# An AFNO kernel: the gathers of the remainder rows of the first two chunks issued by GpSimd instead of SyncE, with the buffers on the right at other addresses

## The chip, the cores and the metric

The kernel runs on one core of a Trainium2 chip. The metric is the time of one execution on the device in microseconds (us), as the median of several executions. Five engines work beside each other and are named as in the profile: PE (TensorE, matmuls), DVE (VectorE), ACT (ScalarE), POOL (GpSimd) and SP (SyncE, which here only issues DMAs). An engine works through its instructions in program order; semaphores tie the engines and the DMAs to one another.

## What is computed

One block of a network on x of 4096 positions and 640 channels (f32): layer norm with a scale and shift taken from a condition vector c, a spectral mixing (AFNO: Fourier transform over the positions, a two-layer complex MLP on the channels of each frequency, soft shrink, inverse transform), and then a SwiGLU feed-forward part. Shortened:

```python
mod = (silu(c) @ w_mod).reshape(1, 6, 1, -1)          # sa, ca, ga, sb, cb, gb
h = layernorm(x) * (1 + ca) + sa
z = rfft2(h over (1, 4096)).reshape(..., 4, 160)      # 4 blocks of 160 channels
hr = relu(z.real @ w1[0] - z.imag @ w1[1] + b1[0])
hi = relu(z.imag @ w1[0] + z.real @ w1[1] + b1[1])
o_r = softshrink(hr @ w2[0] - hi @ w2[1] + b2[0], 0.01)
o_i = softshrink(hi @ w2[0] + hr @ w2[1] + b2[1], 0.01)
x = x + ga * irfft2(o_r + 1j * o_i)
h = layernorm(x) * (1 + cb) + sb
x = x + gb * ((silu(h @ w_gate) * (h @ w_up)) @ w_down)   # 640 -> 1728 -> 640
```

## The kernel before

**Stages.** The AFNO part takes up to about 340 us of the execution, the feed-forward part the rest. The transform of 4096 points is split in two steps, A and B, with a reordering through memory between them. In step A eight tiles t of x (`xa0` to `xa7`, in the pool `xp` on the right side of the on-chip memory) are normalised and multiplied by the first transform's matrix. The results overwrite the `xa` tiles. Step B works on eight chunks ch of frequencies. Chunk 0's tile `g0` is moved directly from the `xa` tiles (`move_g`, L313 to L315, some of these DMAs on POOL); for the others the `xa` tiles are copied in bulk to DRAM (`write_s1`, L353 to L355) and read back as `g1` to `g7` (`load_g`, L301 to L310) along with a table `tb` (`load_tb`).

**A chunk.** For a chunk, `stage_b` (L593) makes step B's matmuls in five groups of 128 channels, t = 0 to 4. The first four groups hold the first 128 channels of each of the four blocks; the fifth holds the 32 channels that remain of each block, four times 32. `evac_b` (L602) takes each group out of PSUM as two parts, a rounded high half by ACT (L606) and the low half by DVE (L607), in a tile `z{ch}_{t}`. The matmuls of the first MLP layer want a block's 32 remaining rows in another arrangement: real and imaginary, high and low half beside each other on 128 partitions. `move_r` (L615 to L619) makes that by four DMAs of 128 KB, one for each block, from `z{ch}_4` into the tile `rz{ch}`. `stage_l1` (L621, matmuls at L646) is the first layer of one block: weights `w1a` and `w1b` on `z{ch}_{b}`, `w1c` on `rz{ch}`. For chunk 0, block 0 all products with `w1a` and `w1b` are issued ahead of the first with `w1c`. ACT and DVE make the high and low halves `h` of the result (L656 to L658), and `u` and `r` of its remainder. `stage_l2` (L682, matmuls at L698) is the second layer with `w2a`, `w2b` and `w2c`, one block behind the first. The inverse transform follows (`stage_i`, L734) and its results go to DRAM by DMAs of POOL (L748, from tiles `co`).

**The second layer's weights** are also split in high and low halves: `weights_high` (ACT at L282, or POOL at L280), `weights_low` (DVE, L285) and `weights_rest` (POOL, L527, the low half as a difference). Each of `w2a`, `w2b` and `w2c` is made in two pieces by several of these. They lie in the pool `p2` on the right, in the place that the `xa` tiles had before, so writing them has to wait for the copies out of the `xa` tiles that lay there.

**What sets the order.** In the AFNO part the order is that of the code (a manual schedule), on every engine. SP issues almost all DMAs, and each of its DMAs uses one of eight semaphores in turn and waits for the DMA eight places before it, so that at most eight are under way. At the place in question the code has, in this order: the bulk copies of the tiles (L490 to L505, with `load_g(1)` and `load_tb(1)` among them), loads of `idn` (L507), `tx` (L508) and `bx` (L530); `stage_b` of chunk 0 for t = 4, 0 and 1; two `weights_high` on ACT; `evac_b(0, 4)`; `move_r(0)` (L774); `evac_b` of t = 0 and 1; the rest of the second layer's weights; and then a loop over p = 4 ch + b, in which `stage_l1` of one block, `stage_b` and `evac_b` of the next chunk, and `stage_l2` of the block before follow one another. `z1_4` and `move_r(1)` come at p = 2.

```python
evac_b(0, 4)
move_r(0)
for b in range(2):
    evac_b(0, b)
weights_low(*prep2[0])
weights_rest(1)
for n in (2, 3):
    weights_high(*prep2[n], pool)
weights_rest(3)
weights_high(*prep2[5], pool)
weights_rest(5)
```

Here `prep2` lists the pieces of the weights: 0 and 1 are of `w2a`, 2 and 3 of `w2b`, 4 and 5 of `w2c`. After the AFNO part, the feed-forward part is put in order by a planner; its instructions are the same before and after.

Of the kernel before, what the change touches and what calls it, by code (L numbers as in the profile page):

```python
# [6 lines left out]
F32 = mybir.dt.float32  # L7
F32R = mybir.dt.float32r
# [5 lines left out]
P = 128  # L14
D = 640
# [157 lines left out]
def body(tc, x, w1, b1, w2, b2, wg, wu, wd, c, wm, k_fa, k_tb, k_tx, k_bm, k_bx, k_ga, k_ge, k_id, out, dbg=None):  # L173
    nc = tc.nc
    pe, act, dve, pool = nc.tensor, nc.scalar, nc.vector, nc.gpsimd
    mm = pe.matmul

    def f32(ap):
        return ap.bitcast(F32)
# [21 lines left out]
    with ExitStack() as top:  # L201
# [35 lines left out]
        with ExitStack() as af:  # L237
            wp = af.enter_context(tc.tile_pool(name="wp", bufs=1, side="right"))
            w1a = wp.tile([P, NB, 640], F32R, tag="w1a", name="w1a")
            w1b = wp.tile([P, NB, 640], F32R, tag="w1b", name="w1b")  # L240
            w1c = qp.tile([P, NB, 640], F32R, tag="wq", name="w1c")
            bm = wp.tile([P, 2, 64], F32, name="bm")
            tx = wp.tile([P, 2], F32, name="tx")
            lp = af.enter_context(tc.tile_pool(name="lp", bufs=1))
            fa = lp.tile([P, 130], F32, name="fa")
# [244 lines left out]
            hp = af.enter_context(tc.tile_pool(name="hp", bufs=1, reuse_waits="tile"))  # L490
# [18 lines left out]
            p2 = af.enter_context(tc.tile_pool(name="p2", bufs=1, side="right", reuse_waits="tile"))  # L509
# [75 lines left out]
            zs = {}  # L585
            pbs = {}
            rzs = {}
            hss = {}

            def width(ch):  # L590
                return 258 if ch == CE else 256
# [9 lines left out]

            def evac_b(ch, t):  # L602
                pb = pbs[ch, t]
                z = lp.tile([P, 2, 2, 258], F32R, tag="z" if t < 4 else "zr", bufs=4 if t < 4 else 1, name=f"z{ch}_{t}")
                zs[ch, t] = z
                act.activation(z[:, 0, :, 0:256], pb, AF.Identity, scale=ca1[:, t:t + 1])  # L606
                dve.scalar_tensor_tensor(z[:, 1, :, 0:256], pb, ca1[:, t:t + 1],  # L607
                                         f32(z[:, 0, :, 0:256]), op0=OP.mult, op1=OP.subtract)
                if ch == CE:
                    pool.tensor_copy(z[:, 0, :, 0:257:256], f32(edge[:, 0, t]))  # L610
                    pool.tensor_copy(z[:, 1, :, 0:257:256], f32(edge[:, 1, t]))
                    pool.tensor_copy(z[:, :, :, 257], zero[:, 0, 0])


            def move_r(ch):  # L615
                rzs[ch] = hp.tile([P, NB, 258], F32R, tag="rz", bufs=2, name=f"rz{ch}")
                NN = width(ch)
                for b in range(NB):
                    nc.sync.dma_start(f32(rzs[ch][:, b, :NN]), f32(zs[ch, 4][32 * b:32 * b + 32, :, :, :NN]))  # L619

            def stage_l1(ch, b):  # L621
                NN = width(ch)
# [148 lines left out]
            for n in (1, 0):  # L771
                weights_high(*prep2[n])
# [4 lines that stand above are left out]
# [31 lines left out]
            def load_first_rows(lo, hi, q, e=slice(0, D)):  # L808
                for k in range(2):
                    q.dma_start(cf[k][lo:hi, :, e], s2[lo:hi, 2 * k:2 * k + 2, e])  # L810
# [4 lines left out]
            for p in range(LAST + 1):  # L815
                ch, b = p // 4, p % 4
# [11 lines left out]
                for q in todo:  # L828
                    stage_b(*q)
                    evac_b(*q)  # L830
                    if q[1] == 4:
                        move_r(q[0])
# [38 lines left out]
                elif p == LAST - 1:  # L871
                    load_first_rows(0, rb - 16, nc.sync)


            def load_first():
                x2 = fx.tile([P, 4, D], F32, tag="gx", bufs=2, name="x2_0")
                nc.sync.dma_start(x2, xv[:, 0:4, :])
                x2s[0] = x2
# [146 lines left out]
        with ExitStack() as ff:  # L1025
# [42 lines left out]
            bufs = {"R": 2, "h1": 1, "wb": 2, "wt": 2, "pc": 4, "px": 2, "gt": 2, "ho": 2, "h32": 1, "gx": 2}  # L1068
# [1324 lines left out]
            mv, rs, _ = fst[3]  # L2393
# [18 lines left out]
            for t in range(NS):  # L2412
                for n in range(NW):
                    if sum_at(n) == t:
                        a, b = sum_w(n)
# [81 lines left out]
```

## Time and profile before

| | us |
|---|---|
| median of 3 executions | 1436.88 |
| lowest and highest of them | 1433.94 and 1438.77 |
| the profiled execution, its own time | 1432.89 |
| the span of its profile | 1431.1 |

The profile is of one execution. Its span runs from the first to the last recorded instruction. A window view cuts the span into stretches and gives for each engine the busy time and, in brackets, the number of instructions; after that the granted clock of PE (1.00 is full speed), the share of the 16 DMA engines' time that was used, and the rate in GB/s. Cut along the kernel's stages:

```profile
0.00:36.00 36.00, 24.75 (x51) 9.69 (x52) 31.05 (x104) 25.52 (x39) 19.94 (x55) 1.00 0.95 375
36.00:60.00 24.00, 22.55 (x94) 13.20 (x92) 20.61 (x41) 18.42 (x35) 16.62 (x18) 1.00 0.90 319
60.00:81.40 21.40, 0.10 (x2) 0.02 (x1) 0.00 (x0) 0.00 (x0) 8.18 (x7) 0.56 0.96 348
81.40:124.00 42.60, 42.60 (x322) 41.91 (x323) 28.05 (x55) 26.34 (x58) 0.00 (x0) 0.94 0.44 125
124.00:340.00 216.00, 213.85 (x1592) 184.21 (x1591) 154.59 (x292) 146.85 (x311) 56.82 (x101) 1.00 0.68 207
340.00:1431.00 1091.00, 1080.57 (x6413) 1046.38 (x6411) 788.40 (x1287) 501.85 (x1019) 517.39 (x517) 1.00 0.80 277
```

The columns are PE, PEld (PE's loading of weights, which runs beside its matmuls), DVE, ACT and POOL. Rows of a timeline give start and duration, engine, line, operation, the tiles `out<-in` without their numbers, shapes, how many instructions are drawn together (x4), and in square brackets the idle time before and what ended it. `SPq` stands for SP's issuing of DMAs, in which the wait for a free semaphore is included; a transfer lands later.

### The profile page before, as it was taken

Reading aid. Unit: us, or ns where it says so; the run is one execution under the profiler, and the core shown is the slowest. Engines: PE = TensorE matmul, PEld = TensorE weight load, DVE = VectorE, ACT = ScalarE, POOL = GpSimd, SP = SyncE. Lnnn points to the kernel's source line nnn. Section 1 sums busy time; section 2 is a strip of 40 time slices with the busy share of each in tenths; the row PEclk is TensorE's granted clock in tenths of the full one; section 3 lists DMA queues with packets and bytes.
Section 4 is the critical chain, followed back from the end, with each engine's and each line's share of the span. In section 5 each row is a group of like instructions: output and inputs, shape, how many; then the busy total and the mean of one; then the engine's idle time right before and its main releaser. Section 6 shows DMA issues by size and latency. Waiting matters only on the chain. (4 is left out here: it accounts for less than half of the span.)

```text
span 1431.1 us, 23688 instructions
## 1 busy us (share of the span) xinstructions
PE 1384.4 (97%) x8466; PEld 1295.4 (91%) x8466; DVE 1022.7 (71%) x1777; ACT 719.0 (50%) x1458; POOL 619.0 (43%) x696
## 2 busy tenths in 40 slices
PE   6679999999999999999999999999999999999998
PEld 2379989967988988899999999999999999999998
DVE  8547666779798698737796848687669757375654
ACT  7547777736555455426463536355255525152441
POOL 5601221137786586416454716345344525052241
PEclk9879999999999999999999999999999999999999
DMA  9956666776698998798968898877999766966634
GB/s 374 330 174 190 210 180 221 196 243 214 222 328 293 338 323 290 273 388 299 341 208 307 319 345 282 296 265 238 368 336 319 233 233 243 348 220 201 205 122 147
DMA packets 175623, 381.35 MB, mean 266 GB/s; under 512 B 22705, under 2 KB 86385, under 8 KB 173490
## 3 DMA queue, kind: packets, MB, share of 16 engines
q1 hardware_dynamic: 166098, 363.55, 73.9%
q0 software_dynamic: 7104, 13.67, 3.3%
q10 hardware_dynamic: 2304, 2.62, 0.5%
q8 instruction: 67, 1.10, 0.3%
q14 instruction: 50, 0.41, 0.1%
HBM read 269.29 MB, written 96.80 MB: 256 GB/s over the span
## 5 line engine op out<-in xcount | busy, mean ns | idle before, releaser
L1400 DVE TENSOR_TENSOR wb<-r,wb 128x768 fp32r<-128x768 f32 (+3 forms) x170 | 174.7, 1038 | 16.1 <-ACT wb L1393 15.8
L2008 PE MATMUL pw<-h,wt 128*128 128x384 f32 x412 | 139.4, 338 | 0.6 <-ACT s_y L2027 0.6
L2010 PE MATMUL pw<-h,wt 128*128 128x384 f32 x412 | 138.3, 336 | 0.0
L2009 PE MATMUL pw<-h,wt 128*128 128x384 f32 x412 | 138.1, 335 | 0.0
L2309 PE MATMUL pc<-wq,L 128*128 128x320 f32 x846 | 132.7, 309 | 0.6 <-DVE x L2266 0.6
L1393 ACT ACTIVATE wb<-r 128x768 fp32r<-128x768 f32 (+3 forms) x168 | 104.6, 639 | 57.0 <-PE pw L2021 41.7
L2068 POOL TENSOR_TENSOR sg<-s_x,sg 128x384 f32<-128x384 f32 x24 | 29.8, 1242 | 234.2 <-DVE s_x L2034 234.2
L2309 PEld LDWEIGHTS pc<-wq,L 128*128 128x128 f32 x846 | 126.3, 188 | 0.8 <-DVE x L2266 0.8
L2088 DVE TENSOR_TENSOR L<-sg,L 128x384 fp32r<-128x384 f32 x144 | 102.9, 738 | 27.4 <-ACT L L2084 26.9
L748 POOL DMA_DIRECT2D s<-co x56 | 33.5, 602 | 185.2 <-ACT co L746 184.6
L2027 ACT ACTIVATE s_x<-pw 128x384 f32<-128x384 f32 x52 | 25.6, 492 | 166.2 <-PE pw L2010 165.2
L2008 PE MATMUL pw<-h,wb 128*128 128x384 f32 x312 | 105.0, 336 | 0.8 <-DVE x L2266 0.8
L2009 PE MATMUL pw<-h,wb 128*128 128x384 f32 x312 | 104.4, 335 | 0.0
L2010 PE MATMUL pw<-h,wb 128*128 128x384 f32 x312 | 104.4, 335 | 0.0
L1931 PE MATMUL pg<-ht,wb 128*128 128x512 f32 x260 | 102.5, 394 | 0.0
L2079 POOL TENSOR_TENSOR sg<-sg,sg 128x384 f32<-128x384 f32 x72 | 92.2, 1280 | 23.2 <-DVE L L2088 19.9
L1932 PE MATMUL pg<-ht,wb 128*128 128x512 f32 x260 | 101.9, 392 | 0.0
L2309 PE MATMUL pe<-wq,L 128*128 128x320 f32 x648 | 101.7, 309 | 0.0
L1933 PE MATMUL pg<-ht,wb 128*128 128x512 f32 x260 | 101.7, 391 | 0.0
L2225 PE MATMUL pd<-wq,a 128*128 128x320 f32 x632 | 96.9, 310 | 0.0
L2309 PEld LDWEIGHTS pe<-wq,L 128*128 128x128 f32 x648 | 96.6, 188 | 0.0
L2225 PEld LDWEIGHTS pd<-wq,a 128*128 128x128 f32 x632 | 93.5, 188 | 0.6
(299 smaller groups left out, 3761.0 us busy)
## 6 DMA issues: line engine op xcount, KB each, us to landing
wq<-wqd SPq DMA_DIRECT2D x83, 640.0 KB, 5.7
wt<-td SPq DMA_DIRECT2D x103, 512.0 KB, 5.4
hs<-ho SPq DMA_DIRECT2D x52, 512.0 KB, 5.6
h<-hs SPq DMA_DIRECT2D x32, 768.0 KB, 7.9
td<-wt SPq DMA_DIRECT2D x25, 512.0 KB, 5.7
r<-in_B_w_gate_dram SPq DMA_DIRECT2D x24, 384.0 KB, 3.5
r<-in_B_w_up_dram SPq DMA_DIRECT2D x24, 384.0 KB, 4.1
xx<-tt SPq DMA_DIRECT2D x28, 320.0 KB, 4.7
```

What stands on the lines that cost most here:

```text
L1393: def high(ks, e=slice(0, c), copy=lambda o, i: act.activation(o, i, AF.Copy)):
L1400: dve.tensor_tensor(wbs[t, n][:, 1, ks, e], raw[t, n][:, ks, e], f32(wbs[t, n][:, 0, ks, e]), op=OP.subtract)
L1931: mm(b, wh, hh, start=(kk == 0), stop=False)
L1932: mm(b, wh, hl, start=False, stop=False)
L1933: mm(b, wl, hh, start=False, stop=(kk == 4))
L2008: mm(b, w(0, kp), a[:, kp, 0], start=start and kp == 0, stop=False, skip_group_check=not start)
L2009: mm(b, w(0, kp), a[:, kp, 1], start=False, stop=False, skip_group_check=not start)
L2010: mm(b, w(1, kp), a[:, kp, 0], start=False, stop=kp == 1, skip_group_check=not start)
L2079: pool.tensor_tensor(o, x, y, op=op)
L2088: dve.tensor_tensor(o[:, 1], raws[j], f32(o[:, 0]), op=OP.subtract)
L2225: mm(b[:, :320], l, m, start=start and i == 0, stop=stop and i == len(s) - 1)
L2309: mm(o[:, :320], ls[q][:, x, k], w[:, q, y], start=start and q == 0 and n == 0, stop=q == 1 and n == 2, skip_group_check=not start)
```

## The change

Four edits. The tile `bm` is allocated four times as wide (2048 bytes for each partition in place of 512) and used as before. The tile `z{ch}_4` moves from the pool `lp` to the pool `hp`, both on the left. The four DMAs of `move_r` are issued by POOL (`pool`) for chunks 0 and 1, and by SP (`nc.sync`) for the others, as before. A tile "spare" of 7680 bytes, which nobody uses, is added to `p2`.

```diff
-            bm = wp.tile([P, 2, 64], F32, name="bm")
+            bm = wp.tile([P, 2, 2, 128], F32, name="bm")[:, 0, 0].rearrange("p (a b) -> p a b", a=2)
...
-                z = lp.tile([P, 2, 2, 258], F32R, tag="z" if t < 4 else "zr", bufs=4 if t < 4 else 1, name=f"z{ch}_{t}")
+                z = (lp.tile([P, 2, 2, 258], F32R, tag="z", bufs=4, name=f"z{ch}_{t}") if t < 4 else
+                     hp.tile([P, 2, 2, 258], F32R, tag="zr", bufs=1, name=f"z{ch}_{t}"))
...
-                    nc.sync.dma_start(f32(rzs[ch][:, b, :NN]), f32(zs[ch, 4][32 * b:32 * b + 32, :, :, :NN]))
+                    (nc.sync if ch > 1 else pool).dma_start(f32(rzs[ch][:, b, :NN]), f32(zs[ch, 4][32 * b:32 * b + 32, :, :, :NN]))
...
+            p2.tile([P, 3 * D], F32, name="spare")
```

The tiles of `p2` now lie 9216 bytes lower: `w2a` ends where `xa1` begins and no longer overlaps an `xa` tile, `w2b` lies over `xa1` and `w2c` over `xa2`; before, the three lay one tile further up, `w2a` over `xa1` too. The tiles of `xp` and `wp` lie 1536 bytes lower. The feed-forward part's tiles keep their addresses. From L604 on, line numbers are one higher in the changed kernel.

SP's instructions around the first two chunks, before the change (`rz_666` and `rz_857` are chunk 0's and chunk 1's remainder rows, `z_4_663` and `z_4_854` the tiles that they are taken from, `xa_118` to `xa_122` tiles of x, `g_892` chunk 2's tile):

```order
L354 DMA s<-xa_118 64x4x640
L354 DMA s<-xa_120 64x4x640
L354 DMA s<-xa_121 64x4x640
L354 DMA s<-xa_122 64x4x640
L507 DMA idn<-in_k_id_dram 128x128
L508 DMA tx<-in_k_tx_dram 128x2
L530 DMA bx<-in_k_bx_dram 128x256
L619 DMA rz_666<-z_4_663 128x1x256 x4
L862 DMA bm<-in_k_bm_dram 128x128
L619 DMA rz_857<-z_4_854 128x1x256 x4
L307 DMA g_892<-s 128x1x2560
L297 DMA tb_894<-in_k_tb_dram 128x512
```

And SP with the change, from the same copy on:

```order
L354 DMA s<-xa_122 64x4x640
L507 DMA idn<-in_k_id_dram 128x128
L508 DMA tx<-in_k_tx_dram 128x2
L530 DMA bx<-in_k_bx_dram 128x256
L863 DMA bm<-in_k_bm_dram 128x128
L307 DMA g_892<-s 128x1x2560
L297 DMA tb_894<-in_k_tb_dram 128x512
```

Eight DMAs have left the queue, four of them from behind the last bulk copy, and the loads for chunk 2 follow `bm` directly. POOL before, from its last DMAs of chunk 0's tile on (`rm_456` and `rr_457` are the weights as loaded, `co_1210` and `co_1296` results of the inverse transform):

```order
L315 DMA g_453<-xa_122 4x4x640 x2
L527 TENSOR_TENSOR w2a<-rm_456,w2a 128x4x160
L280 TENSOR_SCALAR w2b<-rm_456 128x4x160 x2
L527 TENSOR_TENSOR w2b<-rm_456,w2b 128x4x160
L280 TENSOR_SCALAR w2c<-rr_457 128x4x160
L527 TENSOR_TENSOR w2c<-rr_457,w2c 128x4x160
L860 MEMSET zero 128x40
L861 CAST edge<-zero 128x40
L748 DMA s<-co_1210 64x2x320 x2
L748 DMA s<-co_1296 64x2x320 x2
```

POOL with the change, from behind the same DMAs on:

```order
L620 DMA rz_666<-z_4_663 128x1x256 x4
L527 TENSOR_TENSOR w2a<-rm_456,w2a 128x4x160
L280 TENSOR_SCALAR w2b<-rm_456 128x4x160 x2
L527 TENSOR_TENSOR w2b<-rm_456,w2b 128x4x160
L280 TENSOR_SCALAR w2c<-rr_457 128x4x160
L527 TENSOR_TENSOR w2c<-rr_457,w2c 128x4x160
L861 MEMSET zero 128x40
L862 CAST edge<-zero 128x40
L620 DMA rz_857<-z_4_854 128x1x256 x4
L749 DMA s<-co_1210 64x2x320 x2
```

Chunk 0's four moves now stand ahead of the second layer's weights, and chunk 1's between the clearing of `edge` and the transfers of the inverse transform's results. On PE, ACT and DVE the instructions and their order are as before.

## The prediction

> **What bounds the kernel now.** I begin with the page: the span, the busy times, and the slices in time.
>
> ```profile
> span 1431.1 us, 23688 instructions
> PE 1384.4 (97%) x8466; PEld 1295.4 (91%) x8466; DVE 1022.7 (71%) x1777; ACT 719.0 (50%) x1458; POOL 619.0 (43%) x696
> PE   6679999999999999999999999999999999999998
> PEclk9879999999999999999999999999999999999999
> ```
>
> TensorE is busy for 97% of the span, and only the first slices of 36 us are not full. So there is little to win behind them, and a microsecond won early is won at the end, as long as nothing else comes late. What PE waits for is in the view of waits, which lists for each pair the total, the number and the longest:
>
> ```profile
> PE pl L646 <- DMA rz<-z: 21.3, 1, 21.3
> PE pa L438 <- ACT xa L417: 9.9, 2, 8.1
> PE py L1646 <- DVE chl L1636: 2.0, 1, 2.0
> ```
>
> One wait of 21.3 us stands out, for rz, the remainder rows that the change moves. All later waits are of 2.0 us at most. PE's timeline shows its two ends, and SP's timeline shows what stood ahead of the move (start, duration, engine, line; SPq is SP issuing DMAs):
>
> ```profile
> 59.67 0.40 PE L646 MATMUL pl<-z,w1b 128*128 128x256 f32 x2
> 81.38 1.44 PE L646 MATMUL pl<-rz,w1c 128*128 128x256 f32 x5 [21.30 <-DMA rz<-z]
> ```
>
> ```profile
> 60.09 3.27 SPq L310 DMA_DIRECT2D g<-s  x4
> 63.41 0.57 SPq L297 DMA_DIRECT2D tb<-in_k_tb_dram  x1
> 64.03 10.62 SPq L354 DMA_DIRECT2D s<-xa  x10
> 74.69 1.37 SPq L507 DMA_DIRECT2D idn<-in_k_id_dram  x1
> 76.10 1.20 SPq L508 DMA_DIRECT2D tx<-in_k_tx_dram  x1
> 77.41 1.19 SPq L530 DMA_DIRECT2D bx<-in_k_bx_dram  x1
> 78.70 2.57 SPq L619 DMA_DIRECT2D rz<-z  x4
> 81.32 0.59 SPq L862 DMA_DIRECT2D bm<-in_k_bm_dram  x1
> ```
>
> PE stops at 60.07 and goes on at 81.38. The four moves of chunk 0 are issued from 78.70 on, and PE starts 2.7 us after the first of them. SP's issues take long where it has to wait for the eighth DMA before: ten of L354 take 10.62 us. What the moves read was ready much sooner, by VectorE's timeline:
>
> ```profile
> 55.79 0.29 DVE L285 SCALAR_TENSOR_TENSOR w1c<-rr,w1c 128x128 fp32r<-128x128 f32 x1
> 56.34 2.53 DVE L607 SCALAR_TENSOR_TENSOR z<-pb,ca,z 128x512 fp32r<-128x512 f32 x3 [0.26 <-ACT z L606]
> ```
>
> The first of these three is the low half of z0_4, done at 56.34 + 2.53/3 = 57.2. For 21.5 us (57.2 to 78.7) the data waited for SP's queue alone. The windows show the chip in that time (columns: PE, PEld, DVE, ACT and POOL busy, then granted clock, DMA share, GB/s):
>
> ```profile
> 70.00:75.00 5.00, 0.00 (x0) 0.00 (x0) 0.00 (x0) 0.00 (x0) 0.00 (x0) 0.50 1.03 405
> 80.00:85.00 5.00, 3.62 (x17) 3.62 (x18) 1.31 (x3) 2.39 (x6) 0.00 (x0) 0.50 0.47 119
> 85.00:90.00 5.00, 5.00 (x37) 5.00 (x37) 4.33 (x8) 4.33 (x10) 0.00 (x0) 0.87 0.02 3
> ```
>
> No engine works from 70 to 75 us. The copies fill the DMA engines at 405 GB/s, and the clock has fallen to 0.50, where it stays for the first microseconds of PE's work.
>
> **The change: the moves of chunk 0.** They leave SP's queue. On POOL they stand behind the four g moves (over at 51) and wait for z0_4 at 57.2 and for one load that landed long before. What four POOL issues cost is shown by another four, and by the lines of L748 and L315, POOL's other DMAs (min, median and max of an issue in ns, then the same of the time to landing in us):
>
> ```profile
> 327.49 2.42 POOL L805 DMA_DIRECT2D s<-cz  x4
> ```
>
> ```profile
> L748 POOL DMA_DIRECT2D s<-co x56: 594/594/837, 124.4 to 308.2; - x56
> DMA to landing us min/median/max: 2.5/4.6/8.6
> ```
>
> ```profile
> L315 POOL DMA_DIRECT2D g<-xa x4: 572/586/828, 48.2 to 50.4; - x4
> DMA to landing us min/median/max: 3.3/3.6/4.0
> ```
>
> So POOL issues from 57.2 to 59.6. The nearest row for landing is L315's, 10 us earlier beside the same traffic: 3.6 us, so the first block's rows are there at about 61 and one more each 0.6 us. With L748's worst, 8.6, it is 65.8. PE's stall then shrinks from 21.3 us to about 1, **by this wait alone**.
>
> **What is late next.** POOL's next work is the preparation of the second layer's weights, and it now stands behind these moves. Its timeline before:
>
> ```profile
> 54.37 3.12 POOL L527 TENSOR_TENSOR w2a<-rm,w2a 128x640 fp32r<-128x640 f32 x1 [3.35 <-ACT w2a L282]
> 59.00 4.06 POOL L280 TENSOR_SCALAR w2b<-rm 128x640 fp32r<-128x640 f32 x2 [1.51 <-DMA s<-xa]
> 63.14 1.53 POOL L527 TENSOR_TENSOR w2b<-rm,w2b 128x640 fp32r<-128x640 f32 x1
> 64.64 1.81 POOL L280 TENSOR_SCALAR w2c<-rr 128x640 fp32r<-128x640 f32 x1
> 66.53 1.53 POOL L527 TENSOR_TENSOR w2c<-rr,w2c 128x640 fp32r<-128x640 f32 x1
> ```
>
> Before, w2a's rest ran at 54.37, ahead of z0_4, and all was done at 68.1, inside PE's stall. Now it begins at 59.6. VectorE is nearly free of other two-input work there, so I take w2a's rest at the 1.53 of the other two: 61.1; w2b's two highs 4.06: 65.2; w2b's rest 1.53, w2c's high 1.81, w2c's rest 1.53: the **floor is 70.1**. The 3.12 of w2a's rest came beside VectorE's L285 instructions, which read two tiles of SBUF each and ran back to back until 56.08, while the same operation took 1.53 with VectorE idle. In the new order POOL's last three run beside VectorE's work on chunk 0. At the worst each of its instructions holds POOL up: 4.33 us by the window from 85 to 90, where the same work stood; **ceiling 70.1 + 4.33 = 74.4**. I take 72.8, that is w2b's rest at 3.12 (71.7) and a quarter of the 4.33, because most of VectorE's work there reads PSUM or only one tile.
>
> [...]
>
> What PE has to do up to the first matmuls that need w2c's rest is measured:
>
> ```profile
> 89.47 0.46 PE L698 MATMUL pc<-w2c,r 128*128 128x320 f32 x2
> 93.45 1.95 PE L599 MATMUL pb<-tb,g 128*128 128x128 f32 x16
> ...
> 104.94 0.40 PE L646 MATMUL pl<-rz,w1c 128*128 128x256 f32 x2
> ```
>
> From 81.38 to the second of the two at 89.6 it took 8.2 us, most of it at the clock of 0.50. Started at 61.0, PE stands there at 69.2 or sooner, ahead of POOL's 72.8 (and of its floor). So **the new limit is POOL's w2c**, and PE passes that point at 72.8 in place of 89.6: 16.8 us earlier. The moves may even land at 64.6 without cost, since 64.6 + 8.2 = 72.8.
>
> **The clock.** After 81.38 the clock stayed low until some point in the window from 85 to 90: at 0.87 mean, with 0.50 before, that is 1.3 us of it, or 86.3. So 4.9 us ran at half speed, which costs 2.5, and that lay ahead of 89.6. In the new order PE works at 61, then waits again some 4 to 7 us for POOL, and the slow stretch may fall behind the wait. Bounds 0 and 2.5; I take 1.7, nearer to the row, as the wait is shorter than the 21 us that the row followed. Gain: 16.8 − 1.7 = **15.1 us**; with the bounds, 89.6 − 74.4 − 2.5 = 12.7 to 19.5.
>
> **The moves of chunk 1** and what stands behind them:
>
> ```profile
> 96.05 2.51 SPq L619 DMA_DIRECT2D rz<-z  x4
> 98.80 0.52 SPq L307 DMA_DIRECT2D g<-s  x1
> ```
>
> SP issued them at 96.05, when z1_4 was there (SP had waited since 82). With the shift z1_4 comes at 79.3; POOL is free since 72.8; it issues until 81.7, and the last, begun at 81.1 and landing after L748's median of 4.6, is there at 85.7, and PE uses the first at 104.94 − 16.8 = 88.1. Hidden, by 2.4 us or more. The g load of chunk 2 no longer stands behind them and goes out at 82 in place of 98.8, earlier by as much as PE is. Chunk 1's g, issued from 60.09, and its table at 63.41 now share the DMA engines with 0.5 MB of moves, 1.3 us at 405 GB/s. PE needs them at 93.45 − 16.8 = 76.7, and the four loads and the table are issued by 64.0, so they have 12 us. The s<-co transfers behind them on POOL begin at 124.4; shifted, 107, long after rz1 is issued.
>
> **The addresses.** The tiles on the right move down, so w2a's operations no longer wait for the copies out of xa1, and w2b's and w2c's wait for earlier copies: POOL waited 1.51 us at 59.00 for such a copy, and is now past that point only at 61.1. Worth between 0 and 1.5, beside the move nothing on its own: 0, and a little safety for the sum. Instructions on PE, ACT and VectorE keep their order; that costs nothing.
>
> **The sum.** The profiled execution took 1432.89 us, 1.8 more than its span: 1432.89 − 15.1 = 1417.8. It is 4.0 below the median of 1436.88, so by the median 1421.8. I forecast **1421.5**.
>
> **Rivals.** (a) *POOL is quicker or the clock stays*: w2c at 70.1 to 71.5, little lost at low clock, gain 17.5 to 19.5, 1417.4 to 1419.4. For it: VectorE is half idle there. Against it: the 3.12 row. (b) *The moves land late behind the copies*: they go through the same 16 DMA engines, at 405 GB/s until about 80. From a landing at 64.6 on, each microsecond late costs one: at 72, gain 7.7, 1429; at 80, 89.6 − 88.2 = 1.4, 1435.5, no change. For it the full share of 1.03; against it L315's 3.3 to 4.0 beside such traffic. If the wait in SP's queue were not what held the moves, the same no change would follow; the idle 21.5 us since z0_4 speak against it. (c) *Slower: the queue of POOL accepts the moves only as the copies drain*, so that POOL stands in its four issues, with w2's preparation behind. The preparation takes 72.8 − 59.6 = 13.2 us; from issues ending after 89.6 − 13.2 = 76.4 the kernel loses, and at 82, when the copies are through, it is 5.6 us slower: 1442.5. That needs 6 us for an issue; the largest row is 0.84.
>
> [...]
>
> **How the numbers follow.** Forecast (gain 12.7 to 17.5) 0.68; (a) 0.14; (b) partly late, gain 4.3 to 12.7, 0.10; (b) wholly late or nothing done 0.05; (c) 0.03. About 0.3%, 4.3 us, is what a measurement of this kernel can tell from no change. So faster is 0.68 + 0.14 + 0.10 = 0.92, same 0.05, slower 0.03. The range: at the fast end the lowest run of before with the full gain, 1433.94 − 19.5 = 1414.4; at the slow end half of (b), a gain of 8, 1428.9. The rest, some 0.13, is left out.
>
> **What would show it.** In the new profile: POOL's four L620 at 57 to 60; PE's wait for rz at 1 to 5 us in place of 21.3; a new wait of PE, or of ACT or VectorE on whose results it waits, on POOL's w2b or w2c near 70; low clock after it; the later chunks shifted by 15 us with no new wait. Wrong is the forecast if rz lands after 66, if POOL's issues take over a microsecond, or if the shift at chunk 1 is not found again at the end.

## The result, and the profile after

The changed kernel takes 1416.65 us in the median of 4 executions (1413.85 to 1419.23), the kernel before on the same chip 1436.43 (1433.94 to 1438.77). The ratio is 0.9862, with a 95% interval from 0.9836 to 0.9888: 19.8 us less, where 15.1 were forecast. The profiled execution took 1413.85.

The page of the changed kernel begins so:

```profile
span 1412.1 us, 23694 instructions
PE 1383.9 (98%) x8466; PEld 1293.7 (92%) x8466; DVE 1027.9 (73%) x1777; ACT 720.4 (51%) x1458; POOL 622.6 (44%) x704
PE   7899999999999999999999999999999999999998
PEclk9999999999999999999999999999999999999999
```

PE's busy time is what it was (1384.4 before), and the span is 19.0 us shorter: waiting has gone, not work. The first three slices of about 36 us are fuller. PE's waits, again in total, times and longest:

```profile
PE pl L647 <- DMA rz<-z: 2.4, 1, 2.4
PE py L1649 <- DVE chl L1639: 2.0, 1, 2.0
...
PE pc L699 <- POOL w2c L527: 1.4, 1, 1.4
```

The wait for rz is 2.4 us in place of 21.3, and a new one has come, for POOL's last operation on w2c. PE's timeline shows both, and that this execution was about 1 us late even ahead of the place that the change touches. First chunk 0's first matmuls before, then the changed kernel's rows:

```profile
54.45 2.92 PE L599 MATMUL pb<-tb,g 128*128 128x128 f32 x24 [0.37 <-DMA g<-xa]
```

```profile
55.46 2.92 PE L599 MATMUL pb<-tb,g 128*128 128x128 f32 x24 [0.92 <-DMA rr<-in_A_w_dram]
...
63.53 0.86 PE L647 MATMUL pl<-rz,w1c 128*128 128x256 f32 x5 [2.43 <-DMA rz<-z]
...
70.01 0.41 PE L699 MATMUL pc<-w2c,r 128*128 128x320 f32 x1 [0.45 <-POOL w2c L280]
71.83 0.46 PE L699 MATMUL pc<-w2c,r 128*128 128x320 f32 x1 [1.42 <-POOL w2c L527]
...
77.29 1.95 PE L599 MATMUL pb<-tb,g 128*128 128x128 f32 x16
```

The second w2c product stands at 71.83, where it stood at 89.6: 17.8 us sooner. The row with sixteen matmuls of chunk 1 stands at 77.29 in place of 93.45: 16.2 sooner. So 1.6 us are given back in between. The windows of the changed kernel show why (columns as in the section on the profile before; the clock is the third figure from the end):

```profile
68.70:72.10 3.40, 1.53 (x9) 1.05 (x9) 3.37 (x5) 1.61 (x4) 3.25 (x4) 1.00 0.89 330
72.10:75.50 3.40, 3.40 (x16) 3.40 (x16) 2.41 (x5) 0.42 (x1) 0.03 (x1) 0.50 1.03 406
75.50:79.00 3.50, 3.50 (x33) 3.50 (x32) 1.31 (x3) 2.69 (x6) 0.00 (x0) 1.00 1.03 405
```

Behind the wait for w2c PE works for 3.4 us at half clock. From 16.2 at 77 us the lead grows to 19.0 at the end. The larger part of that is a stretch of half clock in the feed-forward part that the profile of before has and this one lacks. It stands behind the wait of 2.0 us for chl, which both have. First the window of before, then that of the changed kernel:

```profile
340.00:350.00 10.00, 8.03 (x31) 6.40 (x30) 9.71 (x12) 4.17 (x7) 4.17 (x3) 0.83 0.95 313
```

```profile
340.00:350.00 10.00, 10.00 (x48) 8.42 (x47) 9.45 (x15) 5.57 (x9) 8.17 (x8) 1.00 0.39 122
```

A mean of 0.83 over 10 us is 3.4 us at 0.50, worth 1.7 us of PE's time. The remaining 1.1 us come in small pieces.

### The profile page after: what moved, and what is told of

The parts are those of the page before. It is cut to its first block, busy times and chain, and to the rows that moved or that the text cites. A ratio compares the mean times of both kernels' runs of the same rounds, so it can differ in the third digit from the quotient of the medians.

```text
span 1412.1 us, 23694 instructions
## 1 busy us (share of the span) xinstructions
PE 1383.9 (98%) x8466; PEld 1293.7 (92%) x8466; DVE 1027.9 (73%) x1777; ACT 720.4 (51%) x1458; POOL 622.6 (44%) x704
## 5 line engine op out<-in xcount | busy, mean ns | idle before, releaser
L1403 DVE TENSOR_TENSOR wb<-r,wb 128x768 fp32r<-128x768 f32 (+3 forms) x170 | 171.7, 1021 | 13.6 <-ACT wb L1396 13.5
```

The source lines that it names most:

```text
L1403: dve.tensor_tensor(wbs[t, n][:, 1, ks, e], raw[t, n][:, ks, e], f32(wbs[t, n][:, 0, ks, e]), op=OP.subtract)
```

## The experiments

The times in one table; the change itself was run twice more beside other kernels.

| kernel | median, us | kernel before beside it | ratio, 95% interval |
|---|---|---|---|
| e1, the change again | 1415.40 | 1434.33 | 0.9876 (0.9854 to 0.9897) |
| e2, moves only | 1418.23 | 1434.33 | 0.9892 (0.9874 to 0.9910) |
| e3, addresses only | 1433.07 | 1434.33 | 0.9994 (0.9983 to 1.0004) |
| e4, chunk 0 only | 1415.41 | 1434.33 | 0.9867 (0.9848 to 0.9886) |
| e5, moves last on POOL | 1421.34 | 1434.27 | 0.9917 (0.9897 to 0.9938) |
| e6, rest of w2a first | 1413.48 | 1434.27 | 0.9860 (0.9843 to 0.9877) |
| e7, early on SP | 1414.88 | 1434.27 | 0.9865 (0.9843 to 0.9887) |
| e8, wait for w2c filled | 1414.60 | 1434.27 | 0.9863 (0.9848 to 0.9878) |
| e9, as e6, wait for rz filled | 1417.98 | 1432.66 | 0.9894 (0.9876 to 0.9913) |
| e10, as e7, wait for rz filled | 1418.06 | 1432.66 | 0.9891 (0.9874 to 0.9908) |
| e11, the change beside e9, e10 | 1417.05 | 1432.66 | 0.9882 (0.9862 to 0.9902) |
| e12, as e10, half filled | 1413.89 | 1433.77 | 0.9878 (0.9853 to 0.9904) |

Medians of one kernel differ from set to set (the change: 1415.40 to 1417.05, the kernel before: 1432.66 to 1436.43), so steps of one or two microseconds are read from the traces, of which there is one for each run.

### e1: the change once more

> The changed kernel once more, for a second profile. My sum: the wait for rz gives about 18.9 us, the low clock before the second layer's first products gives 2.1 back to the good, the new wait for POOL's w2c costs 1.9 and the low clock behind it 1.2, and 2.6 us of the gain come later than 340 us, where one stretch of half clock of 3.4 us (1.7 us of work) was in the profile of before and not in that of the change. If that stretch belongs to the change, it is missing again here, and the kernel before has it whenever it is profiled; if it falls by chance, the gain up to 110 us is again 16 to 17 us and only the part behind varies by 0 to 3 us. Time 1414 to 1419 us.

The waits up to 110 us are the same to a tenth (2.3 for rz, 1.4 for w2c), with half clock again for one stretch right behind the wait for w2c (0.50 from 72.4 to 75.8). In the feed-forward part the stretch is not at 340 but at 512, by the window from 510 to 520 of this run:

```profile
510.00:520.00 10.00, 8.43 (x49) 8.40 (x50) 6.70 (x13) 4.23 (x8) 7.37 (x11) 0.83 0.97 337
```

It is there in e4 and e11 too (0.83 each in the same window); in e3, whose AFNO part waits as before, there is none between 340 us and the last microsecond (its mean granted clock is 0.992, that of the profile of before 0.990). The changed kernel's own two profiles differ in it (none in the first, one in e1). So this stretch does not belong to the change: it comes and goes between executions, 1.7 us each time.

### e2: the moves alone

```diff
-                    nc.sync.dma_start(f32(rzs[ch][:, b, :NN]),
+                    (nc.sync if ch > 1 else pool).dma_start(f32(rzs[ch][:, b, :NN]),
```

This is the only edit made to the kernel before.

> The moves of chunks 0 and 1 on POOL, all addresses as before. Theory of the prediction: the addresses are worth 0 to 1.5 us, so 1416 to 1418 us and no wait that the changed kernel does not have. Rival: with the old addresses the first tile of results of the second layer (tt0_0) lies over xa5, whose last copy is the eighth of the ten late bulk copies and lands at about 81 us; with PE 17 us earlier this wait of DVE at L700 is no longer covered: DVE stands from 74 to about 81, PE waits about 3 us for a free PSUM bank at its next second-layer products (L698), and the time is 3 us above that of the changed kernel, about 1419.5.

The rival holds. PE's two longest waits in the first part of e2, then DVE's:

```profile
PE pc L698 <- DVE tt L700: 3.4, 1, 3.4
PE pl L646 <- DMA rz<-z: 2.8, 1, 2.8
```

```profile
DVE tt L700 <- DMA s<-xa: 8.2, 1, 8.2
```

DVE's timeline in e2, and PE's:

```profile
74.48 0.42 DVE L678 SCALAR_TENSOR_TENSOR r<-u,r 64x256 fp32r<-64x256 f32 x1
83.07 0.89 DVE L700 TENSOR_TENSOR tt<-pc,b2t 128x320 f32<-128x320 f32 x2 [8.17 <-DMA s<-xa]
```

```profile
83.62 1.17 PE L698 MATMUL pc<-w2a,h 128*128 128x320 f32 x3 [3.37 <-DVE tt L700]
```

DVE's first addition into the second layer's result tile (`tt0_0`, L700) stands for 8.2 us, because with the old addresses that tile lies in part over xa5, and the eighth of the ten late bulk copies reads xa5. With the new addresses it lies over xa4, whose last copy is the second of the ten: there the same addition still waits for a copy, 0.4 us in the changed kernel and 2.0 in e1, and PE for none of it. PE has two PSUM banks for these products; both are full, so it stands 3.4 us, and a second stretch of half clock follows: the three products in the row above take 1.17 us, where such three take 0.69 in the kernel before (at 95.16). The medians differ by 2.8 us (1418.23 against 1415.40); their ratios' intervals overlap, so the time alone does not settle it, but the wait in the trace does. In the kernel before, this addition came only at 90.75 us, and without a wait: the wait for rz had covered it.

```profile
90.75 0.89 DVE L700 TENSOR_TENSOR tt<-pc,b2t 128x320 f32<-128x320 f32 x2
```

### e3: the addresses alone

```diff
-                    (nc.sync if ch > 1 else pool).dma_start(f32(rzs[ch][:, b, :NN]),
+                    nc.sync.dma_start(f32(rzs[ch][:, b, :NN]),
```

This is the changed kernel with its moves put back on SP.

> All addresses as in the change, the moves on SP as before. Theory: nothing is gained as long as PE waits for rz until 81 us, because POOL's weights and the results' tiles are ready by then with either addresses: the time of before, within 0.3% (1432 to 1441 us), with the wait for rz at 21 us. Rival, the addresses alone start something earlier (POOL's 1.5 us wait gone, copies or loads sooner): a time 1.5 us or more below before and a shorter wait for rz.

The ratio is 0.9994, and PE waits for rz as long as before:

```profile
PE pl L647 <- DMA rz<-z: 22.0, 1, 22.0
```

POOL's wait of 1.5 us ahead of w2b is gone, and nothing comes of it. The addresses are worth nothing alone, and 2.8 us of the medians together with the moves (e1 against e2). The address edits were run only together. By the layout it is the spare tile that takes `tt0_0` from xa5: it moves `p2` against the `xa` tiles by its 7680 bytes, while `bm` moves both alike. A run with the spare tile alone beside the moves is missing.

### e4: chunk 0 alone

```diff
-                    (nc.sync if ch > 1 else pool).dma_start(
+                    (nc.sync if ch > 0 else pool).dma_start(
```

> As the change, but only chunk 0's moves on POOL; those of chunk 1 stay on SP, ahead of chunk 2's loads. Theory: chunk 0's moves give the whole gain; SP has its bulk copies issued by about 82 us, issues chunk 1's moves then, and they land at 85 to 88, at the edge of their first use at 88: within 1 us of the changed kernel, 1416 to 1418 us. Rival: chunk 1's moves land behind the last bulk copies at 88 to 92, and PE has a new wait for rz of 1 to 4 us near 88: 1418 to 1421 us.

1415.41 us, the time of e1, with no new wait for rz. Chunk 1's moves are hidden on either queue.

### e5: the moves behind POOL's weights

```diff
             evac_b(0, 4)
-            move_r(0)
             for b in range(2):
                 evac_b(0, b)
...
             weights_rest(5)
+            move_r(0)
```

> As the change, but chunk 0's moves are issued by POOL behind all of the second layer's weights in place of ahead of them. My theory is that the moves and POOL's weights are two chains of about the same end and that who goes first is worth as much as the one makes the other wait: POOL's weights end at about 68 as before, the moves are issued at 68 to 70.5, the first lands 3.6 to 5 later at 72 to 73, and PE needs 6.5 to 8 us from there to the second w2c product: 79 to 81, against 71.5 in the changed kernel. Time 8 to 10 us above the change: 1423 to 1426 us; no wait for w2c is left. Rival, POOL's weights are no bound and only the queue of SP mattered: within 2 us of the change.

POOL is through with w2c at 67.0 and then issues the moves; PE stands 9.1 us for them and for nothing of w2:

```profile
66.90 2.30 POOL L620 DMA_DIRECT2D rz<-z  x4
```

```profile
PE pl L647 <- DMA rz<-z: 9.1, 1, 9.1
```

The second w2c product comes at 80.0, as worked out (79 to 81). The time is 1421.34, about 6 us above the change where 8 to 10 were expected. That expectation took the distance to the change's 71.5 whole into the time, but the execution saves the stretch of half clock behind w2c (three products with w2b take 0.60 us at 80.56, where the change's take 1.00 at 72.89): chunk 1's row stands at 83.81, 6.5 us behind the change's. Direction and mechanism hold. In the change the moves with PE's work behind them end at 69.6, where PE comes to w2c, and the weights at 71.8; what goes first on POOL sets what PE waits for.

### e6: the rest of w2a ahead of the moves

```diff
+            weights_rest(1)
             evac_b(0, 4)
             move_r(0)
             for b in range(2):
                 evac_b(0, b)
             weights_low(*prep2[0])
-            weights_rest(1)
```

> As the change, but the rest of w2a is done by POOL ahead of the moves, in the 6.5 us in which POOL waits for z0_4. If POOL's chain behind the moves is what PE waits for, its end goes from 71.1 (of the second profile) down by the 1.6 us that w2a's rest takes: w2c's rest ends at about 69.5, PE's wait for it of 1.4 shrinks to below 0.3, and the second w2c product comes 1.2 to 1.6 us sooner; the clock may then stay up too, another 1.2. Time 1412.5 to 1415. Rival, POOL is not the bound there, or the rest runs into z0_4 and delays the moves: 0 to 1 us slower than the change.

The wait for POOL's w2c is gone; a wait of 0.4 us for DVE's part of w2c is left. But the second w2c product stands at 71.84, no sooner than with the change, while chunk 1's row stands at 75.74, 1.5 us sooner than the change's 77.29:

```profile
63.73 0.84 PE L647 MATMUL pl<-rz,w1c 128*128 128x256 f32 x5 [2.42 <-DMA rz<-z]
...
71.84 0.38 PE L699 MATMUL pc<-w2c,r 128*128 128x320 f32 x1 [0.43 <-DVE w2c L285]
...
75.74 1.95 PE L599 MATMUL pb<-tb,g 128*128 128x128 f32 x16
```

In e6 the half clock comes earlier, behind the wait for rz and so ahead of the w2c product; in the change it comes behind it. Past both, the gain that was expected is there in the trace. The median, 1413.48 us, is in the expected range, but the interval of its ratio overlaps the change's, so the times do not settle it. The windows of e6:

```profile
61.70:65.10 3.40, 1.37 (x12) 1.37 (x13) 0.00 (x0) 0.83 (x3) 3.32 (x3) 1.00 1.01 294
65.10:68.50 3.40, 3.40 (x19) 3.40 (x18) 3.36 (x5) 3.32 (x9) 3.32 (x3) 0.50 0.95 315
```

### e7: the moves on SP, ahead of the late copies

```diff
+            stage_b(0, 4)
+            evac_b(0, 4)
+            move_r(0)
             load_g(1, range(4))
             load_tb(1)
...
-            for b, tag in ((4, None), (0, None), (1, "p2")):
+            for b, tag in ((0, None), (1, "p2")):
...
-            evac_b(0, 4)
-            move_r(0)
```

The functions that these lines call stand ahead of them, and only chunk 1's moves are on POOL.

> As the change, but chunk 0's moves are issued by SP again, now ahead of chunk 1's g loads and of the last ten bulk copies; to have z0_4 there in the program, its matmuls and its evacuation stand ahead of them too, and on ACT ahead of w2a's high halves. Theory: it is the place in the queue that counts, not which engine issues: SP issues them at 57 to 60, they land 3 to 5 us later at 61 to 64, POOL's weights are done at 68 to 69 with no moves ahead of them, and PE comes to the second w2c product at 69 to 70: 1412.5 to 1416 us. Rival, DMAs on SP's queue are slow because of the copies that are still under way: they land at 66 or later, PE waits for rz 5 us or more, 1416 to 1420.

SP issues them at 60.1, and PE goes on at 63.48, within a tenth of the changed kernel:

```profile
60.11 2.74 SPq L532 DMA_DIRECT2D rz<-z  x4
```

```profile
63.48 0.86 PE L650 MATMUL pl<-rz,w1c 128*128 128x256 f32 x5 [2.75 <-DMA rz<-z]
```

The time is 1414.88 us. So here it is the place in a queue that counts, not which engine issues: SP serves as well as POOL when the moves are not behind the ten late copies. On SP the first lands about 3.4 us after its issue (60.11 to 63.48); on POOL it took 5.1 (58.40 to 63.53). POOL's w2c is done at 66.9, PE does not wait for it, and chunk 1's row stands at 74.85. That is 2.4 us sooner than in the change, of which 1.3 are an earlier start of chunk 0 (54.15 against 55.46).

### e8: the wait for w2c filled

```diff
                     for i, (l, m) in enumerate(seq):
+                        if not (ch or b or q) and i == 6:
+                            idle(12)
                         mm(pc[:M, :W], l, m, start=(i == 0), stop=(i == len(seq) - 1))
```

> As the change, with twelve matmuls more that nothing uses, issued by PE just ahead of the first products with w2c, where PE otherwise waits 1.9 us for POOL. Theory: the stretch of half clock behind that wait comes from the wait; the twelve matmuls take 1.6 us of it, the clock stays up, and the 1.2 us that PE loses at half clock behind it come back, as the shift at 75 us against that at 72 us shows: 0 to 1.2 us below the change, at the edge of what the runs can tell; the clock in the profile decides. Rival, the clock falls for another reason (the wait for rz before): it falls at the same place, and the time is the same or up to 0.5 us longer.

Inconclusive for the question that it asked. The stretch of half clock fell behind the wait for rz this time (64.1 to 67.5 us by the trace's clock), ahead of the filled place. And the twelve calls came out as 24 matmuls, 2.84 us together and more than the wait of 1.9, so that PE passed the second w2c product only at 73.4.

### e9, e10 and e12: the wait for rz filled

In e6 and e7, ahead of the first products with rz:

```diff
                     for o, n in ((0, 6), (1, 6), (2, 4)):
                         products(o, 0, n)
+                    idle(18)
```

> As e6 (the rest of w2a ahead of the moves), with 18 matmuls more that nothing uses between chunk 0's first products and those with rz, where PE waits 2.4 us. In the change, e1, e6, e7 and e8 alike one stretch of half clock of 3.4 us fell behind whichever of the two early waits took up more than half of a stretch of 3.4 us before; so taking away the wait for w2c alone (e6) or filling it (e8) only moved that stretch to behind the wait for rz. Theory: with both gone (the wait for w2c by order, that for rz by filling) no stretch of half clock is left before 340 us, PE passes the second w2c product at 70 to 70.6 in place of 71.8, and the time is 1 to 2 us below the change, 1412.5 to 1414.5. Rival: the fall of the clock has nothing to do with these waits, and one stretch is there again.

> As e7 (the moves on SP, ahead of the late copies), with the same 18 matmuls in the wait for rz. Theory: as e9, no half clock before 340 us; POOL's weights are done at 67 and no wait for them is left, so PE passes the second w2c product about 1.7 us sooner than in e7: 1 to 2 us below e7, 1412 to 1414 us, which would be the fastest of all. Rival: as in e9, and then the time of e7.

Both show what was expected of the clock: by the trace there is no half clock until the last two microseconds (mean granted clock 0.999 and 1.000). Neither gained by it: here too each call made two matmuls, the filling took 4.2 us, and PE came to the products with rz at 65.8 without a wait, later than in e6 and e7 (63.7 and 63.5). A part of that is a later start of chunk 0 (at 56.4 and 55.5 against 55.7 and 54.2). Counted from there to chunk 1's row, e9 took 20.0 us and e6 20.1, e10 20.6 and e7 20.7: what the clock gave went into the filling. The medians are 1417.98 and 1418.06. The last run halves the filling.

> As e10 with half as many filling matmuls: in e9 and e10 each of the 18 came out as two on the engine, so that they took 4.2 us, 1.4 us or more longer than the wait that they were to fill, while the clock stayed up as expected. With 9 they take 2.1 us of e7's wait of 2.8. Theory: no stretch of half clock before 340 us, a wait for rz of about 0.7 left, and from the first product with rz to the second w2c product 6.4 us as in e10, against 7.8 in e7: 1.4 us below e7's profile up to that point, 1411 to 1416 us in the median, with the runs' spread of some 2 us over that. Rival: the rest of the wait is enough to let the clock fall, and the 7.8 us are there again.

The clock stays up (1.00 in the windows) and the wait for rz that is left is 1.1 us. Windows of e12, at the places where it could have fallen:

```profile
61.00:64.40 3.40, 2.58 (x23) 2.38 (x22) 0.00 (x0) 0.00 (x0) 3.32 (x3) 1.00 0.90 255
64.40:67.80 3.40, 3.13 (x26) 3.13 (x27) 1.42 (x2) 2.54 (x7) 3.32 (x2) 1.00 0.99 304
```

From the first product with rz to the second w2c product it took 6.9 us (64.67 to 71.52), 0.5 of it a wait for DVE's part of w2c, against 7.6 in e7 (63.48 to 71.05): 0.7 us won, half of what was expected. At 1413.89 us and a ratio of 0.9878 it is not to be told from the change, and neither are e6 and e7. From chunk 0's first matmul to chunk 1's row the traces of e6, e7 and e12 (20.1, 20.7 and 20.4 us) are 1 to 2 us shorter than the change's four (21.7 to 21.9), but no version shown here beats the change's median by more than the measurement is uncertain.

### e11: the change beside them

> The changed kernel beside e9 and e10, on the same chip and with the same runs of before: 1414 to 1417 us, with one stretch of half clock at 72 us.

As expected but for the stretch's place, 73.1 us, and a time at the upper edge: 1417.05, with 2.2 and 1.4 us as the two waits.

## Why the prediction came out as it did

**The bound.** That PE's wait for rz was a wait in SP's queue is shown: put ahead of the late copies on POOL (the change) or on SP (e7), the moves take it from 21.3 to 2.4 or 2.8 us. The 1 us that was forecast for it was too little. The first landing took 5.1 us, not L315's 3.6 (4.4 for L315's own in this profile). That cost nothing at this point, as the forecast had said of landings up to 64.6: PE came to w2c at 69.6 and stood there for 1.9 us all the same.

**What is late next.** The new limit is POOL's w2c, as forecast, at 71.8 where 72.8 was taken. POOL's rows after the change, term for term with the sum:

```profile
58.40 2.24 POOL L620 DMA_DIRECT2D rz<-z  x4 [6.91 <-DVE z L608]
60.61 1.60 POOL L527 TENSOR_TENSOR w2a<-rm,w2a 128x640 fp32r<-128x640 f32 x1
62.13 3.65 POOL L280 TENSOR_SCALAR w2b<-rm 128x640 fp32r<-128x640 f32 x2
65.86 1.70 POOL L527 TENSOR_TENSOR w2b<-rm,w2b 128x640 fp32r<-128x640 f32 x1
67.51 2.44 POOL L280 TENSOR_SCALAR w2c<-rr 128x640 fp32r<-128x640 f32 x1
70.04 1.74 POOL L527 TENSOR_TENSOR w2c<-rr,w2c 128x640 fp32r<-128x640 f32 x1
```

The chain took 13.4 us from z0_4 on (58.40 to 71.78), against 15.6 in the sum (57.2 to 72.8) and 12.9 at its floor. The term that was too large is above all w2b's rest, 1.70 and not 3.12 (1.57 to 1.75 in e1, e4 and e11): VectorE's run of L285 instructions, beside which the 3.12 stood, did not stand beside it, though VectorE was busy for 1.46 of the 1.70 us. The 1.1 us that were added for VectorE's other work, a quarter of 4.33 chosen by what its instructions read, were my estimate: no run shows that this sets how long they hold POOL up. In their place the runs show 0.6 more on w2c's high (2.44 for 1.81) and 0.2 on its rest (1.74 for 1.53). The chain began 1.2 us later than in the profile of before, which took back about half of the error. VectorE too had a long instruction there, by its rows for h from 60 to 75 us (min, median and max in ns):

```profile
L659 DVE TENSOR_TENSOR h<-h,h x4: 419/426/1751, 64.9 to 70.3; 128x256 fp32r<-128x256 f32 x4
```

One of these subtractions, 0.42 us otherwise, took 1.75 from 70.3 on, while POOL's w2c rest ran from 70.04 to 71.78. What made the two longer is not shown. ACT waited 2.1 us for VectorE's next result, PE for none of it.

**The clock.** 1.7 us were taken for the half clock, and 1.6 were lost between 72 and 77 us. The place was forecast; that the size fits is luck in part. It was chosen between 0 and 2.5 for a wait of 4 to 7 us, and PE's wait at w2c was 1.9: less than the forecast's own 72.8 − 69.2 = 3.6, because PE came there later and POOL was done sooner.

**The sum.** Up to the second w2c product 17.8 us in place of 16.8, half clock 1.6 in place of 1.7: 16.2 by chunk 1, where 15.1 was forecast. In e1 chunk 1's row stands 16.9 us sooner (76.59), and the span is 16.9 us shorter. Chunk 0 began 0.5 to 1.9 us later than before in the four profiles of the change, e1, e4 and e11; counted from its first matmul to chunk 1's row, the way is 39.0 us before and shorter by 17.1 to 17.4 in all four. That is the mechanism's own gain. Whether the later start belongs to the change or to the execution is not shown. The rest of the profile's 19.0 us lies behind chunk 1: 1.7 for the stretch that the profile of before happened to have, and 1.1 in small pieces. It is not shown to be the change's, and neither is the step from there to 19.8, since the medians' difference is 18.9 us in e1's set and 15.6 in e11's. By size the result, 1416.65, lies just beyond rival (a)'s 1417.4 to 1419.4, but by (a)'s reason only in part: POOL was a little quicker than forecast, though w2c came at 71.8 and not at 71.5 or sooner, and the clock was not kept.

**Chunk 1** was hidden, as forecast (e4).

**The addresses: here the prediction was wrong.** Its step reads that they were "worth between 0 and 1.5, beside the move nothing on its own", and the sum had them at 0 since POOL's wait for the copies was covered. It looked at the weights in `p2` only. The result tiles `tt` lie in the same pool, and with the old addresses DVE's first write to one waits for a copy near the very end of the bulk. In the kernel before that wait was hidden behind the same 21.3 us that the moves take away. e2 shows it open: 8.2 us on DVE, 3.4 on PE, a second stretch of half clock, and 2.8 us in the median. Since the change makes both edits, the forecast time came out right without it.

**The rivals.** (b) did not come about: the moves landed at 63.5 beside the full traffic (a DMA share of 1.01 from 60 to 65 us). (c) neither: an issue took 0.56 us (2.24 for four). That other tiles than rz's were behind the copies was a rival that I had not listed.

## What to carry to other kernels

When one long wait goes, list every wait that ended during it, on all engines and for all tiles that share the freed space, and ask for each where it stands in the new time: an edit can be worth nothing alone (e3) and some microseconds beside another (e2 against e1). An urgent small transfer belongs ahead of the bulk in whatever queue it is issued from; here the issuing engine mattered less than what stood ahead of the issue and behind it (e5, e7). And a gain that leaves PE with a wait elsewhere can be given back in part by the clock: here 1.6 us of 17.8.

## What the runs showed of the hardware

The half clock came in stretches of 3.41 us or several of them on end. In the changed kernel it was one (72.07 to 75.48); in the kernel before 23.89 us, seven times as long (62.39 to 86.28), and one more of 3.41 (345.69 to 349.11).

In windows of 3.40 us right ahead of such a fall PE was idle for more than half of the time: it was busy for 1.53 in the changed kernel (the row from 68.70), for 1.64 in e1 (from 69.00), for 1.37 in e6 (from 61.70), for 0.92 in e7 (from 61.00) and for 1.08 in the kernel before (from 59.00). At 1.77 the clock stayed up, but at 1.51 it did so too, in the stretch with the wait for chl. Both rows are the changed kernel's, the first with the whole tail of the wait for rz in it:

```profile
61.90:65.30 3.40, 1.77 (x15) 1.77 (x16) 0.35 (x1) 1.23 (x4) 3.40 (x3) 1.00 0.99 291
324.65:328.06 3.41, 1.51 (x8) 0.98 (x6) 3.41 (x3) 1.37 (x2) 2.75 (x2) 1.00 0.95 280
```

So these traces show no sharp limit. Cut into stretches of 3.41 us in step with the half clock, the profiles of the two kernels show it fall behind 1.11 and 1.44 us of PE's work (before, from 58.97 and 342.28) and behind 1.54 (the change, from 68.65), and stay up behind 1.51 (the change, from 324.65) and 1.59 (before, from 28.25); why is open. Waits of 1.9 us (for w2c in the change) and of 2.4 (for rz in e6), neither longer than a stretch, each had the half clock behind them. In the change, e1 and e11 it was the wait for w2c (1.9, 1.8 and 1.9 us), in e6, e7 and e8 that for rz (2.4, 2.8 and 2.2). What decides between the two is not shown: the code of e8 and e11 is the same up to there and both wait 2.2 us for rz; the clock fell behind it in e8 and not in e11.
